# The last product of a fused attention and two-FFN kernel on scaled 16-bit parts, its third batch with seven products for eight

## Chip, cores and metric

The kernel runs on one core of one Trainium2 chip. The metric is the device time of one execution in microseconds; lower is better. Three runs of the kernel before took 1029.26, 1030.34 and 1037.39 us (median 1030.34).

## The reference, cut to what matters

```python
B, H, S, D = 4, 8, 576, 64                 # attention, batch by batch
x = attention_with_memory(q, k, v, M_prev, z_prev, beta)      # (2304, 512)
h = ((x @ w1) * (x @ w2)) @ w3             # 512 -> 1024 -> 1024
x2 = h @ w_out                             # 1024 -> 512
hg = sigmoid(x2 @ w_gate) * (x2 @ w_val)   # 512 -> 1536
out = hg @ w_out2                          # 1536 -> 512, float32
```

The result must hold to float32, so each product is made of parts: an operand is split into a high part and the small rest, and three matmuls are summed (high with high, low weight with high, high weight with low).

## The kernel before, in words

The work goes batch by batch (four of 576 tokens; a row of a result is a tile of 128 features by 576 tokens, in two halves of 288). Weights are converted from 64-bit integers once, in batch 0; w3 and w_out are first multiplied into one matrix. Each batch then has four stages. "ab": eight rows f of `x@w1` and `x@w2`, multiplied into `h`. "xw": four rows of `x2`. "gv", the gate stage: twelve rows of the gate and value products, joined with a sigmoid into `hg`. "ot", the output stage: four rows d, each two halves of 12 feature blocks times 3 matmuls (`prod`, L467), so 4 x 2 x 12 x 3 = 288 matmuls of 288 columns a batch, on 4-byte parts (float32 rounded for TensorE, "fp32r"). The attention of the next batch is woven in between the matmuls of ab, xw and ot by `drive` (L1109), not in gv; batch 3 has none left.

The parts are 4-byte in batch 0. The weights of ab and gv are split again into two 16-bit parts ("late" work, `late_split`, L279): each conversion task loads a raw copy from DRAM into a tile `wraw`, multiplies it by a power of two (`split_scaled`, L174: ACT writes the high part, DVE the rest) and stores it. "P" tasks make plain parts, "S" tasks first form four sums of blocks (`sums`). Batches 2 and 3 use these sums in `two_rows` (L509): seven block products in place of eight (`prod2`, L478), each six matmuls of 288 columns, added up by DVE, ACT and POOL. How often a task's step comes is set by `PACE`, one step in so many calls of `pump`; tasks that a load needs are forced (`late_until`).

Weights reach TensorE through a ring of five tiles `wslot` (`load_step`, L382), loaded by SP's queue in the order of the list `again`; in the third pass the three `wraw` tiles serve as more places. Accumulators: three banks `ps_f`, and four others that the attention uses. PE's order is that of the program (a manual schedule); DVE, ACT, POOL and SP are put in order by a scheduler with its own time model.

The rows of `hg` are split into 4-byte parts by `split_rows` (L569): an ACT cast and a DVE or POOL subtraction. The output row is copied by ACT (L758) and stored by one DMA:

```python
for k in range(F2):
    prod(ps[:, :HS], slot(s + k // 4), k % 4, hs[k], c0, k == 0, k == F2 - 1)
...
nc.scalar.copy(osb[:, c0 : c0 + HS], ps[:, :HS])
```

Of the kernel before, what the change touches and what calls it, by code (L numbers as in the profile page):

```python
# [54 lines left out]
FRAC = 0.96  # L55
FA = (1.0, 0.6)
FR0 = (0.75, 1.0)
PACE = (5, 4, 4, 14, 4)
# [5 lines left out]
def tile_attention_memory_ffn(  # L64
# [35 lines left out]
    mcol = cp.tile([128, NJ + 2 * B], BF16, name="mcol")  # L100
# [20 lines left out]
    def behind(ins):  # L121

        if "pe" in paced:
            tc.add_manual_dep(
                ins.ins,
                paced["pe"].ins.name,
                mybir.DependencyInfo(mybir.DependencyClass.NoSync, mybir.DependencyReason.DATA),
                reason="pace",
            )
# [35 lines left out]
    def total(col, name):  # L165
        n = col.shape[1]
        ps = ps_f.tile([128, 512], F32, tag="f", name=name)
        nc.tensor.matmul(ps[:, :n], ones, col, start=True, stop=True)
        return ps[:, :n]

    def largest(dst, src, axes):
        nc.vector.tensor_reduce(dst, src, axes, ALU.max, apply_absolute_value=True)
# [61 lines left out]
    NTHIRD = len(again)
    again += second
# [12 lines left out]
    done = []  # L248

# [25 lines left out]
    def late_scales():  # L275
        power(wsc[:, :NJ], wsc[:, NJ:], total(mcol[:, :NJ], "wsum"))
        nc.vector.tensor_reduce(wmax, wtop.rearrange("p d f -> p f d"), AX.X, ALU.max)

    def late_split():  # L279
# [5 lines left out]
        m = jobs.index(u)  # L285
        by = wsc[:, m : m + 1]
        raw = raws[n]

        def made(x):
            d = whole16[u][x]  # L290
            nb = d.shape[2]
# [3 lines left out]
            nc.sync.dma_start(out=d, in_=t)  # L295
# [34 lines left out]
    def conv_step():  # L330
# [27 lines left out]
        elif ws["step"] == 1:  # L358
# [3 lines left out]
            nc.vector.scalar_tensor_tensor(z, y, 3, tmp["r"], ALU.logical_shift_left, ALU.bitwise_or)  # L362
            if hf == 1 and u in kept:
                nc.sync.dma_start(out=kept[u], in_=raws[u])
            if hf == 1 and u in whole16:
                n = jobs.index(u)
                largest(mcol[:, n : n + 1], raws[u], AX.XY)
# [14 lines left out]
    def load_step():  # L382
# [3 lines left out]
        src, key, nb = again[m]  # L386
        late = m - NTHIRD
# [3 lines left out]
        while key is not None and key not in done:  # L391
            late_until(ws["task"] + 1)
        n = ws["ring"]
        if key is not None:
            w = fp.tile([128, 2, nb, 128], F16, tag=tag, name=f"wslot{n}", bufs=bufs)
            nc.sync.dma_start(out=w, in_=src[:, :, :nb])
        else:
            w = fp.tile([128, 2, 4, 128], F32R, tag=tag, name=f"wslot{n}", bufs=bufs)
            nc.sync.dma_start(out=w.bitcast(F32), in_=src)
        put(tag, [w])  # L400
# [74 lines left out]
    def prod2(ps, w, blk, x):  # L475
        for k in range(2):
            for part, (wi, xi) in enumerate(((0, 0), (1, 0), (0, 1))):
                paced["pe"] = nc.tensor.matmul(  # L478
                    ps, w[:, wi, blk + k, :], x[:, xi, k, :],
                    start=k == 0 and part == 0, stop=k == 1 and part == 2,  # L480
# [4 lines left out]
    def token_steps(name, x01, x23, ops, scale):  # L485
        both = {}
        b11, b12 = x01[:, :, :HS], x01[:, :, HS:]
        b21, b22 = x23[:, :, :HS], x23[:, :, HS:]
# [759 lines left out]
```

## Time and profile before

| | us |
|---|---|
| median of three runs | 1030.34 |
| the profiled execution | 1028.78 |
| its span, first to last instruction | 1026.8 |
| PE busy in the span | 1000.1 |
| DVE, ACT, POOL busy | 684.5, 571.8, 247.4 |

The trace is that of one execution. PE is TensorE's matmuls, PEld its weight loads, DVE VectorE, ACT ScalarE, POOL GpSimd, SP the engine that issues DMAs. A matmul's own duration contains its way through the array; how fast matmuls follow each other is read from a run of them, its length over its count.

### The profile page before, as it was taken

What the parts mean: (1) busy time and instruction counts of PE and PEld (TensorE: products, weight loads), DVE (VectorE), ACT (ScalarE), POOL (GpSimd) and SP (SyncE); (2) the same over time, 40 slices, a digit from 0 to 9 for tenths busy, and PEclk for the clock granted to TensorE, in tenths of its full rate; (3) what the DMA queues carried; (4) which work ended last, traced back from release to release, by engine and by line L of the source; (5) the groups of instructions that cost most, each with busy time, mean ns of one, the idle gap of its engine ahead of it and who ended that gap; (6) DMA issues with size and microseconds to landing.
All of it is one profiled execution on the core that took longest, in us unless ns stands there. A gap on an engine that the chain in (4) does not pass through costs nothing.

```text
span 1026.8 us, 19856 instructions
## 1 busy us (share of the span) xinstructions
PE 1000.1 (97%) x7382; PEld 834.0 (81%) x7382; DVE 684.5 (67%) x1596; ACT 571.8 (56%) x1179; POOL 247.4 (24%) x246
## 2 busy tenths in 40 slices
PE   7999999999999998999999999899999999999998
PEld 3556787888999898898977788677877888897798
DVE  6865888778776627765566659998877427837730
ACT  7977786567777635654455444455644433235420
POOL 3454021212000201321101012453244302403420
PEclk9989999999999999999999999999999999999999
DMA  8865799857776479863777588655755335545551
GB/s 294 249 214 197 260 345 314 307 193 262 243 248 223 159 252 372 293 201 99 266 245 243 207 282 311 187 182 162 226 179 187 112 112 190 196 150 162 186 193 56
DMA packets 80376, 224.83 MB, mean 219 GB/s; under 512 B 10520, under 2 KB 22936, under 8 KB 80280
## 3 DMA queue, kind: packets, MB, share of 16 engines
q1 hardware_dynamic: 80280, 223.57, 64.2%
q8 instruction: 58, 0.95, 0.4%
q14 instruction: 38, 0.31, 0.1%
HBM read 165.34 MB, written 58.20 MB: 218 GB/s over the span
## 4 chain that ended last, share of the span: by engine, by line
PE 76%; DVE 6%; ACT 2%; issue 1%; DMA 1%; POOL 0%; SPq 0%; DVEq 0%; ACTq 0%; POOLq 0%
PE gv L467 14%; PE ot L467 14%; PE gvp L478 12%; PE ab L467 9%; PE xw L467 9%; PE abp L478 6%; PE s L902 3%; PE t L963 3%; PE o L1031 3%; PE o L1016 1%; PE wps L467 1%; PE o L1024 1%; DMA wraw<-kf 1%; DVE p L907 1%; PE qt L1000 0%
## 5 line engine op out<-in xcount | busy, mean ns | idle before, releaser
L478 PEld LDWEIGHTS <-wslot 128*128 128x128 f16 x1680 | 163.0, 98 | 47.3 <-issue 5.9
L933 POOL TENSOR_SCALAR p<-p,sm,omg 116x116 f32<-116x116 f32 (+4 forms) x100 | 87.3, 877 | 325.4 <-DVE sm L931 187.2
L467 PE MATMUL ot<-hg,wslot 128*128 128x288 f32 x1152 | 165.7, 299 | 0.0
L467 PEld LDWEIGHTS ot<-hg,wslot 128*128 128x128 f32 x1152 | 154.5, 188 | 6.5 <-issue 5.5
L467 PE MATMUL gv<-x,wslot 128*128 128x288 f32 (+1 forms) x1152 | 147.5, 290 | 0.2 <-ACT gsb L134 0.2
L478 PE MATMUL gvp<-x,wslot 128*128 128x288 f16 x1008 | 124.3, 286 | 1.1 <-DVE x L177 1.1
L467 PE MATMUL ab<-x,wslot 128*128 128x288 f32 x768 | 121.0, 308 | 0.2 <-DVE wpart L597 0.2
L134 ACT ACTIVATE p<-p,sm 116x116 f32<-116x116 f32 (+4 forms) x160 | 92.9, 583 | 43.7 <-DVE sm L907 43.5
L467 PE MATMUL xw<-h,wslot 128*128 128x288 f32 x768 | 113.7, 300 | 2.4 <-ACT h L570 1.1
L467 PEld LDWEIGHTS ab<-x,wslot 128*128 128x128 f32 x768 | 107.2, 193 | 7.9 <-issue 5.0
L467 PEld LDWEIGHTS xw<-h,wslot 128*128 128x128 f32 x768 | 103.6, 188 | 7.4 <-issue 3.0
L907 DVE CUSTOM_DVE_ANT_0 p<-s,msk 116x116 f32<-116x116 f32 (+4 forms) x160 | 67.9, 454 | 36.1 <-PE s L902 35.5
L478 PE MATMUL abp<-x,wslot 128*128 128x288 f16 x672 | 87.4, 286 | 1.7 <-DVE c11ab L544 1.2
L572 DVE TENSOR_TENSOR wslot<-wraw,wslot 128x512 fp32r<-128x512 f32 x76 | 56.1, 740 | 40.3 <-ACT wslot L570 40.0
L467 PEld LDWEIGHTS gv<-x,wslot 128*128 128x128 f32 x576 | 76.4, 188 | 0.5 <-ACT gsb L134 0.5
L963 PE MATMUL t<-idf,p 116*116 116x116 f32 x480 | 67.6, 270 | 6.4 <-DVE p L933 3.9
L963 PEld LDWEIGHTS t<-idf,p 116*116 116x116 f32 x480 | 53.6, 137 | 20.7 <-issue 5.2
L467 PEld LDWEIGHTS <-wslot 128*128 128x128 f16 x576 | 56.3, 98 | 14.2
L353 ACT ACTIVATE cy<-r 128x512 f32<-128x512 f32 x76 | 51.3, 675 | 12.0 <-DVE wraw L362 2.4
L570 ACT CAST wslot<-wraw 128x512 fp32r<-128x512 f32 x76 | 47.0, 620 | 17.3 <-PE gv L467 7.4
L362 DVE SCALAR_TENSOR_TENSOR wraw<-cy,cr 128x512 int32<-128x512 int32 x76 | 54.0, 738 | 2.5 <-ACT cr L354 2.3
L981 ACT COPY pt<-t 116x696 f32<-116x696 f32 (+2 forms) x74 | 47.2, 647 | 9.5 <-PE t L963 9.2
(156 smaller groups left out, 1550.5 us busy)
## 6 DMA issues: line engine op xcount, KB each, us to landing
wslot<-k SPq DMA_DIRECT2D x76, 512.0 KB, 4.2
wslot<-ka SPq DMA_DIRECT2D x40, 512.0 KB, 4.0
k<-wslot SPq DMA_DIRECT2D x36, 512.0 KB, 3.7
wraw<-kf SPq DMA_DIRECT2D x32, 512.0 KB, 6.6
wslot<-kb SPq DMA_DIRECT2D x40, 384.0 KB, 3.9
r<-in_gv_dram SPq DMA_DIRECT2D x24, 512.0 KB, 5.2
kf<-wraw SPq DMA_DIRECT2D x20, 512.0 KB, 3.2
ka<-wS SPq DMA_DIRECT2D x20, 512.0 KB, 4.9
```

Source lines behind the costliest of these rows:

```text
L134: ins = nc.scalar.activation(**kw)
L353: nc.scalar.activation(out=y, in_=hi, func=AF.Prelu, scale=2.0**-112, alpha=2.0**32)
L362: nc.vector.scalar_tensor_tensor(z, y, 3, tmp["r"], ALU.logical_shift_left, ALU.bitwise_or)
L467: paced["pe"] = nc.tensor.matmul(ps, w[:, wi, blk, :], x[:, xi, cols : cols + n], start=first and part == 0, stop=last and part == 2,)
L478: paced["pe"] = nc.tensor.matmul(ps, w[:, wi, blk + k, :], x[:, xi, k, :], start=k == 0 and part == 0, stop=k == 1 and part == 2,)
L570: nc.scalar.copy(dst[:, 0], src)
L572: eng.tensor_sub(dst[:, 1], src, dst[:, 0].bitcast(F32))
L902: nc.tensor.matmul(os_[hh], q_[r, 0, i * T : (i + 1) * T], k_[r, 1, c0:c1], start=x == 0, stop=x == len(terms) - 1,)
L907: nc.vector.tensor_tensor_reduce(out=ps_[hh][:, c0:c1], in0=os_[hh], in1=msk[:, SP - w + c0 : SP - w + c1], scale=-0.125, scalar=3.0e38 if ...
L933: lower(SHARE_N).tensor_scalar(ps_[hh][:, :w], ps_[hh][:, :w], sm[:, 6 + hh : 7 + hh], omg[:T, 2 * p + hh : 2 * p + hh + 1], ALU.mult, ALU ...
L963: nc.tensor.transpose(tp[:T, c : c + T], src[hh][:, j * T : (j + 1) * T], idf[:T, :T])
L981: nc.scalar.copy(to, got)
```

## The change

The output stage of batches 1, 2 and 3 uses 16-bit parts scaled by powers of two. `w_out2` gets late tasks of its own: six P and six S (named `("o", dp, g)`), whose raw copies are the 12 `ko` stores that take the place of 12 stores of 4-byte parts. The scale of `hg` comes from a bound (`measure`, `hg_scale`), known after gate row 2: one matmul with a column of ones (`hgsum`) and some DVE instructions on single columns. `hg` is split with `split_scaled`, rows 0 and 1 later through a `queue`. In batches 1 and 2 the loop stays plain, and the copy multiplies by the scale back (`oback`); output goes out by halves. In batch 3 `out_rows` makes two pairs of output rows with seven products of three groups g of four feature blocks: 2 x 7 x 3 x 6 = 252 matmuls. The first pair (dp 0) holds seven banks, so that the seven products of group 0, then of group 1, then of group 2 follow each other; its weights lie ready in three tiles `ow` in the attention's old buffers. A group's operands are 11 `token_steps` on tiles 576 wide: seven splits (p0 to p6) and four subtractions (t1 to t4), queued when the group's four rows are done and let go two in a row. `two_rows` also changes in ab and gv: products 2, 7 and 3 are added into the banks of 1, 6 and 5, so that the sum `c11` on DVE becomes an ACT copy (or goes into the sigmoid), and the sum `u4` on POOL goes. The ring stays at five in the third pass.

```diff
-PACE = (5, 4, 4, 14, 4)
+PACE = (4, 4, 4, 14, 4, 8, 4)
...
+tasks = [(u, "P") for u in jobs[:F2]] + [(("o", *x), "P") for x in pairs_of]
+tasks += [(u, "PS") for u in jobs[F2:]]
+tasks += [(u, "S") for u in jobs[:F2]]
+tasks += [(("o", *x), "S") for x in pairs_of]
...
-        tag, bufs = ("wslot", RING) if late < 0 or late % (RING + 3) < RING else ("wraw", 3)
-        if in_use(tag) >= bufs:
+        if in_use("wslot") >= RING:
             return False
...
-        p2 = product(2, 1, 2, 5)
+        product(2, 1, 2, 5, a)
         c11 = tmp_("asb", "c11")
-        nc.vector.tensor_add(c11, p2, s1)
-        gate(c11)
+        if sigmoid:
+            act_fn(out=c11, in_=a, func=AF.Sigmoid, scale=by)
+        else:
+            nc.scalar.copy(c11, a)
...
+        every = ((0, 0), (1, 1), (2, 2), (3, 5), (4, 3), (5, 4), (6, 6))
+        for g in range(2):
+            for i, xo in every if views else every[:3]:
+                product(i, g, xo)
...
+            for t, d in ((pa, o16[0]["P"][:, 0:3]), (pb, o16[0]["S"][:, 0:3]), (pc, o16[0]["S"][:, 3])):
+                behind(nc.sync.dma_start(out=t, in_=d))
...
+            if f < 2:
+                queue.append(lambda: split_tied(ht[:, 0], ht[:, 1], hraw, hgs[:, 0:1]))
+            else:
+                split_scaled(ht[:, 0], ht[:, 1], hraw, hgs[:, 0:1])
...
+                    first = [steps[x] for x in ("p0", "t1", "p1", "t2", "p2")]
+                    then = [steps[x] for x in ("p5", "t3", "p3", "p4", "t4", "p6")]
+                    queue.extend(first + then)
...
+        flush(len(queue))
+        if b == 3:
+            yield from out_rows(b, 0, hs, oback, views)
+            yield from out_rows(b, 1, hs, oback)
...
+                if b:
+                    nc.scalar.activation(out=osb, in_=ps[:, :HS], func=AF.Copy, scale=oback[:, 0:1])
```

First place, DVE at the end of batch 3. Before, its last six instructions finish gate row 11 (`u3`, `u4` sums, `hgraw` the row):

```order
L544 TENSOR_TENSOR c11gv_11_12507<-gvp_11_2_12500,s1gv_11_12478 128x288
L549 TENSOR_TENSOR u3gv_11_12517<-gvp_11_7_12510,u2gv_11_12487 128x288
L553 TENSOR_TENSOR u4gv_11_12498<-gvp_11_3_12519,u4gv_11_12498 128x288
L559 TENSOR_TENSOR u3gv_11_12517<-u3gv_11_12517,gvp_11_4_12529 128x288
L525 SCALAR_TENSOR_TENSOR hgraw_11_12468<-s5gv_11_12496,x2back_11441,u4gv_11_12498 128x288
L525 SCALAR_TENSOR_TENSOR hgraw_11_12468<-u3gv_11_12517,x2back_11441,c11gv_11_12507 128x288
```

Now the list goes on; `hq_8`, `hq_10` are the four quarters of group 2, `hg_1_m`, `hg_2_m` the 16-bit parts of groups 1 and 2 (a tile holds two operands and bears the even or first one's name, so the two rows that write `hg_2_2` are p3 from `hq_8_1`, then p2 from `hq_8_0`):

```order
L181 SCALAR_TENSOR_TENSOR hg_1_6_12530<-hq_6_0_12094,hgs_11876,hg_1_6_12530 128x576
L564 TENSOR_TENSOR hq_8_0_12237<-hq_8_1_12238,hq_8_0_12237 128x576
L181 SCALAR_TENSOR_TENSOR hg_2_5_12543<-hq_10_0_12380,hgs_11876,hg_2_5_12543 128x576
L181 SCALAR_TENSOR_TENSOR hg_2_5_12543<-hq_10_1_12381,hgs_11876,hg_2_5_12543 128x576
L564 TENSOR_TENSOR hq_8_1_12238<-hq_10_1_12381,hq_8_1_12238 128x576
L181 SCALAR_TENSOR_TENSOR hg_2_0_12533<-hq_8_0_12237,hgs_11876,hg_2_0_12533 128x576
L564 TENSOR_TENSOR hq_8_0_12237<-hq_10_1_12381,hq_8_0_12237 128x576
L181 SCALAR_TENSOR_TENSOR hg_2_2_12540<-hq_8_1_12238,hgs_11876,hg_2_2_12540 128x576
L564 TENSOR_TENSOR hq_10_0_12380<-hq_8_0_12237,hq_10_0_12380 128x576
L181 SCALAR_TENSOR_TENSOR hg_2_2_12540<-hq_8_0_12237,hgs_11876,hg_2_2_12540 128x576
L181 SCALAR_TENSOR_TENSOR hg_2_6_12552<-hq_10_0_12380,hgs_11876,hg_2_6_12552 128x576
L670 SCALAR_TENSOR_TENSOR u2ot_0_12655<-otf_2_12558,hgs_11876,s1ot_0_12654 128x288
```

What moved: of the 11 steps of group 2, p2's low part has become the last but one; the queue had it fifth.

Second place, DVE in row 3 of batch 2's ab stage, with the attention's score rows (ISA, `p`, `sm`) between. Before:

```order
L549 TENSOR_TENSOR u3ab_3_8184<-abp_3_7_8167,u2ab_3_8132 128x288
L907 ISA p_0_4_0_8152,sm_0_4_8154<-s_0_4_1_0_8174,msk,sm_0_4_8154 116x290
L907 ISA sm_0_4_8154 116x1
L907 ISA p_0_4_1_8153,sm_0_4_8154<-s_0_4_1_1_8175,msk,sm_0_4_8154 116x290
L907 ISA sm_0_4_8154 116x1
L820 TENSOR_TENSOR qkl_1_8260<-qk_1_7827,qkh_1_8259 128x580
L553 TENSOR_TENSOR u4ab_3_8143<-abp_3_3_8186,u4ab_3_8143 128x288
L525 SCALAR_TENSOR_TENSOR hraw_3_8101<-s5ab_3_8141,undo_7755,u4ab_3_8143 128x288
L377 TENSOR_TENSOR wraw_27_7690<-wraw_27_7690 128x256
L559 TENSOR_TENSOR u3ab_3_8184<-u3ab_3_8184,abp_3_4_8206 128x288
```

Now:

```order
L620 TENSOR_TENSOR u3ab_3_8260<-abp_3_6_8205,s1ab_3_8203 128x288
L1174 ISA p_0_4_0_8229,sm_0_4_8231<-s_0_4_1_0_8250,msk,sm_0_4_8231 116x290
L1174 ISA sm_0_4_8231 116x1
L1174 ISA p_0_4_1_8230,sm_0_4_8231<-s_0_4_1_1_8251,msk,sm_0_4_8231 116x290
L1174 ISA sm_0_4_8231 116x1
L1087 TENSOR_TENSOR qkl_1_8335<-qk_1_7919,qkh_1_8334 128x580
L624 TENSOR_TENSOR u2ab_3_8212<-abp_3_5_8214,u2ab_3_8212 128x288
L594 SCALAR_TENSOR_TENSOR hraw_3_8181<-s5ab_3_8221,undo_7848,u2ab_3_8212 128x288
L433 TENSOR_TENSOR wrawl_7785<-wrawl_7785 128x256
L631 TENSOR_TENSOR u3ab_3_8260<-u3ab_3_8260,abp_3_4_8281 128x288
```

What moved: the pair `u3`, `u4` has become `u3`, `u2`, which no longer wait for a sum on POOL, and `c11ab`, which stood some rows ahead of these, is gone from DVE.

Third place, SP's queue where batch 3 passes from xw (`k`) to gv (`ka`, `kb`: S and P weights). Before:

```order
L396 DMA wslot_11417<-ka_138 128x2048
L396 DMA wslot_11431<-kb_139 128x2x768
L396 DMA wslot_11482<-ka_141 128x2048
L396 DMA wslot_11496<-kb_142 128x2x768
L396 DMA wslot_11544<-ka_144 128x2048
L396 DMA wslot_11558<-kb_145 128x2x768
```

Now, from the first weight of gv on:

```order
L450 DMA wslot_11529<-ka_141 128x2048
L450 DMA wslot_11577<-kb_142 128x2x768
L450 DMA wslot_11591<-ka_144 128x2048
L867 DMA ow_11666<-op_182 128x4608
L867 DMA ow_11667<-os_183 128x4608
L867 DMA ow_11668<-os_183 128x1536
L450 DMA wslot_11640<-kb_145 128x2x768
L450 DMA wslot_11654<-ka_147 128x2048
```

What moved: the three `ow` loads (128 x 4608, 4608 and 1536 elements of two bytes) stand ahead of the weights of gate row 1.

## Rows read from the trace of the kernel before

**Rows 1.** The page's busy times, whole span: busy us (share) and instructions of each engine.

```profile
PE 1000.1 (97%) x7382; PEld 834.0 (81%) x7382; DVE 684.5 (67%) x1596; ACT 571.8 (56%) x1179; POOL 247.4 (24%) x246
```

**Rows 2.** Windows by stage: start:end, length, then as the second line says.

```profile
core 0: us, PE busy (x) PEld busy (x) DVE busy (x) ACT busy (x) POOL busy (x), PEclk, DMA share, GB/s
...
398.00:471.00 73.00, 73.00 (x555) 63.71 (x554) 51.75 (x127) 41.43 (x89) 20.84 (x17) 0.98 0.70 241
...
503.95:574.60 70.65, 70.65 (x579) 56.50 (x577) 48.15 (x80) 37.85 (x54) 4.20 (x3) 1.00 0.73 245
...
574.60:629.20 54.60, 54.60 (x420) 47.99 (x419) 36.47 (x82) 25.17 (x45) 5.17 (x5) 1.00 0.78 269
...
629.20:697.00 67.80, 64.31 (x515) 47.16 (x513) 63.01 (x167) 33.94 (x81) 33.44 (x33) 1.00 0.64 212
...
796.00:855.00 59.00, 59.00 (x455) 51.19 (x453) 25.38 (x77) 26.43 (x55) 11.47 (x10) 1.00 0.37 119
...
922.70:984.80 62.10, 61.81 (x506) 49.23 (x504) 44.79 (x93) 32.31 (x62) 25.25 (x28) 1.00 0.55 183
...
984.80:1026.80 42.00, 38.44 (x291) 38.21 (x288) 1.45 (x4) 4.41 (x10) 1.67 (x2) 1.00 0.31 104
```

**Rows 3.** Timeline of PE, batch 3: start us, duration us, engine, line, operation, tiles, count.

```profile
903.52 0.18 PE L168 MATMUL x2sum<-mcol,ones 128*128 128x1 bf16 x1
...
927.84 57.24 PE L478 MATMUL gvp<-x,wslot 128*128 128x288 f16 x466 [0.29 <-DVE x L177]
...
984.83 38.42 PE L467 MATMUL ot<-hg,wslot 128*128 128x288 f32 x288
```

**Rows 4.** Waits of PE, whole span: total us, times, longest us.

```profile
PE t L963 <- DVE mn L849: 2.4, 1, 2.4
...
PE abp L478 <- DVE c11ab L544: 1.2, 1, 1.2
```

**Rows 5.** Groups of instructions by form, whole span: busy us, mean ns.

```profile
L467 PEld LDWEIGHTS ot<-hg,wslot 128*128 128x128 f32 x1152 | 154.5, 188 | 6.5 <-issue 5.5
...
L478 PEld LDWEIGHTS <-wslot 128*128 128x128 f16 x1680 | 163.0, 98 | 47.3 <-issue 5.9 <-DMA wslot<-k 0.5
...
L177 DVE SCALAR_TENSOR_TENSOR wS<-wraw,wsc,wS 128x1024 f16<-128x1024 f32 x20 | 26.0, 1300 | 5.9 <-ACT wS L176 5.7
...
L177 DVE SCALAR_TENSOR_TENSOR x<-x2f,x2s,x 128x576 f16<-128x576 f32 x14 | 11.1, 818 | 4.7 <-ACT x L176 4.7
...
L380 DVE TENSOR_TENSOR wraw<-wraw 128x256 f32<-128x256 f32 x20 | 9.7, 484 | 0.3
...
L177 DVE SCALAR_TENSOR_TENSOR wP<-wraw,wsc,wP 128x1024 f16<-128x1024 f32 x12 | 16.7, 1402 | 9.5 <-ACT wP L176 9.4
```

**Rows 6.** The same view, DVE in 629.20 to 697.00 us.

```profile
L544 DVE TENSOR_TENSOR c11ab<-abp,s1ab 128x288 f32<-128x288 f32 x8 | 3.6, 447 | 0.2 <-PE abp L478 0.2
```

**Rows 7.** Timeline of DVE at the end of batch 3's gate stage.

```profile
985.19 0.45 DVE L559 TENSOR_TENSOR u3gv<-u3gv,gvp 128x288 f32<-128x288 f32 x1 [0.28 <-PE gvp L478]
...
985.58 0.52 DVE L525 SCALAR_TENSOR_TENSOR hgraw<-s5gv,x2back,u4gv 128x288 f32<-128x288 f32 x1
...
986.01 0.51 DVE L525 SCALAR_TENSOR_TENSOR hgraw<-u3gv,x2back,c11gv 128x288 f32<-128x288 f32 x1
```

**Rows 8.** Groups of DVE by form, 922.70 to 984.80 us.

```profile
L500 DVE TENSOR_TENSOR x2f<-x2f,x2f 128x576 f32<-128x576 f32 x1 | 0.7, 747 | 0.0
```

**Rows 9.** Timeline of DVE between batches 0 and 1; in brackets the idle time before.

```profile
381.74 1.28 DVE L177 SCALAR_TENSOR_TENSOR wP<-wraw,wsc,wP 128x1024 f16<-128x1024 f32 x1 [4.18 <-ACT wP L176]
...
387.67 1.29 DVE L177 SCALAR_TENSOR_TENSOR wP<-wraw,wsc,wP 128x1024 f16<-128x1024 f32 x1 [4.64 <-ACT wP L176]
```

**Rows 10.** DMA: GB/s in 40 slices of the span; issues, KB each, us to landing.

```profile
GB/s 294 249 214 197 260 345 314 307 193 262 243 248 223 159 252 372 293 201 99 266 245 243 207 282 311 187 182 162 226 179 187 112 112 190 196 150 162 186 193 56
...
wraw<-kf SPq DMA_DIRECT2D x32, 512.0 KB, 6.6
```

**Rows 11.** The output copies (tile osb): ns min/median/max, first and last start us.

```profile
L758 ACT COPY osb<-ot x32: 377/399/402, 344.5 to 1023.3; 128x288 f32<-128x288 f32 x32
```

More of the change, by code (lines that the diff above doesn't have):

```diff
@@ L248, in tile_attention_memory_ffn, with flush @@
     done = []
+    queue = []
+    def flush(n):
+        while queue and n > 0:
+            queue.pop(0)()
+            n -= 1
     def in_use(tag):
@@ L479, in prod2, with split_tied, token_steps @@
                     ps, w[:, wi, blk + k, :], x[:, xi, k, :],
-                    start=k == 0 and part == 0, stop=k == 1 and part == 2,
-                )
-    def token_steps(name, x01, x23, ops, scale):
+                    start=not more and k == 0 and part == 0, stop=k == 1 and part == 2,
+                    skip_group_check=more,
+                )
+    def split_tied(hi, lo, src, by, tied=True):
+        a, d = split_scaled(hi, lo, src, by)
+        if tied:
+            behind(a)
+            behind(d, "dve")
+    def token_steps(name, b11, b12, b21, b22, ops, scale, tags, apart=False, tied=False):
         both = {}
-        b11, b12 = x01[:, :, :HS], x01[:, :, HS:]
-        b21, b22 = x23[:, :, :HS], x23[:, :, HS:]
+        t = {1: b11, 2: b11, 3: b12, 4: b21}
         def parts(m, src):
@@ L509, in two_rows, with sub, step @@
-    def two_rows(s, x, name, ht, hraw, by, sigmoid, cost=0.0):
+                    both[m // 2] = fp.tile([128, 2, 2, 2, HS], F16, tag=tags[m // 2], name=f"{name}_{m}", bufs=1)
+                o = both[m // 2][:, m % 2]
+                split_tied(o[:, 0], o[:, 1], src(), scale(), tied)
+                ops[m] = o
+            return step
+        def sub(n, a, b):
+            def step():
+                if apart and n < 3:
+                    t[n] = fp.tile([128, 2, HS], F32, tag="hraw", name=f"{name}_t{n}")
+                ins = nc.vector.tensor_sub(t[n], a(), b())
+                if tied:
+                    behind(ins, "dve")
+            return step
@@ L658, in ffn @@
             x2 = {}
[L659 removed]
+            x2top = fp.tile([128, 8], F32, tag="x2top", name=f"x2top{b}", bufs=1)
+            steps = token_steps(f"x2_{b}", *quarters(*xf), x2, lambda: x2s[:, 0:1], [f"x{n}" for n in range(4)])
             x2s = bound_x2(b, htop)
@@ new lines, in measure @@
+        def measure(f):
+            if f == 0 and b == 1:
+                for d in range(2):
+                    largest(x2top[:, d : d + 1], x2[d][:, 0], AX.X)
+            elif f == 1 and b == 1:
+                for d in range(2, KC):
+                    largest(x2top[:, d : d + 1], x2[d][:, 0], AX.X)
+            elif f == 0:
+                for n, m in enumerate((0, 1, 5, 4)):
+                    queue.append(
+                        lambda n=n, m=m: behind(largest(x2top[:, 2 * n : 2 * n + 2], x2[m][:, 0], AX.X), "dve")
+                    )
+            elif f == 2:
+                return hg_scale(b, x2top[:, : 4 if b == 1 else 8], x2s)
```

403 lines of the change are left out of this document (297 added, 106 removed).

## The prediction

> **What bounds the kernel now.** I read first how busy each engine is, then where TensorE waits, then single stages. PE is busy 1000.1 of 1026.8 us [rows 1]. The windows by stage say the same closer to the change: in batch 1's gate stage (503.95 to 574.60), batch 1's output stage (574.60 to 629.20) and batch 2's output stage (796 to 855) PE has no idle time at all, DVE is busy for 25.4 to 48.2 us of them, and the granted clock is 1.00, that is 2.4 GHz [rows 2]. So these stages last as long as their matmuls take to follow each other, and the first question is what one matmul costs there, not how busy another engine is. What PE waited for is little: the longest single wait, 2.4 us, is a transpose of the attention that waited for DVE just after batch 0 [rows 4]. One stage stands out: 629.20 to 697.00, batch 2's ab stage, where PE idles 3.5 us (67.80 less 64.31) and DVE is busy 63.0 of 67.8 us [rows 2]. There DVE is the bound beside PE.
>
> **The spacing of matmuls.** The timeline of PE in batch 3 has two long runs with nothing between: 466 gate matmuls on 16-bit parts in 57.24 us, 122.8 ns each, and 288 output matmuls on 4-byte parts in 38.42 us, 133.4 ns each; both have 288 columns [rows 3]. The weight load of the 4-byte form lasts 188 ns, longer than that spacing; that of the 16-bit form lasts 98 ns [rows 5]. The Trainium skill, "TensorE: Matmul & The Clock Gate", section "Back-to-back issue gap", gives a warm spacing of N/2.4 + 2.5 ns with no word of the type, 122.5 ns for 288 columns; by that rule new types alone gain nothing here. The 16-bit run agrees with it (122.8), the 4-byte run doesn't (133.4), and the runs decide the sum below.
>
> **The sum, part by part.**
>
> Batches 1 and 2: 288 matmuls each keep their number and lose 133.4 - 122.8 = 10.6 ns each: 3.05 us a batch, 6.1 us. Attention is woven in there and keeps its own matmuls; PE has no idle time to absorb the gain.
>
> Batch 3: 288 x 133.4 = 38.4 us becomes 252 x 122.8 = 30.9 us: 7.5 us less. Together 13.6 us.
>
> Single-column matmuls: three `hgsum`, `osum` and a second `wsum`. The one like them, `x2sum`, lasts 0.18 us [rows 3]; five cost between 0 (overlapped) and 0.9 us. I take 0.4.
>
> Batch 3, the steps of group 2. While gate rows 4 to 11 run, DVE has per row four sums of 0.45 and two products of 0.52 us [rows 7] and two queued steps, each a split of 0.82 [rows 5] or a subtraction of 0.75 [rows 8]: 2.84 + 1.64 = 4.5 us, against 42 x 0.1228 = 5.16 us of matmuls. It keeps up, but steps of group 1 are left over, and the order now puts p2 of group 2 behind nearly everything. DVE read the last gate product 0.36 us after the first output matmul had started (985.19 against 984.83) [rows 3, 7]; product 7 of the last row comes two products of 0.737 us earlier, so DVE can start `u3` 1.11 us before the output stage. From there to the end of p2 the order has 21 instructions: 11 splits (9.0), 5 subtractions (3.75), three sums and two products (2.4), 15.2 us. Two instructions that follow each other overlap a little: 985.58 to 986.01 is 0.43 for one of 0.52 [rows 7]. With 20 x 0.08 off, p2 is done 12.5 us into the stage, without it 14.1. PE wants that part after 16 products and two matmuls, 98 x 0.1228 = 12.0 us. The wait is 0.4 to 2.0 us; I take 1.0. Nothing in the second product pair hides it, since PE's order is fixed and all its matmuls stand behind.
>
> Batch 3, the `ow` loads. They are 128 x 10752 elements of two bytes, 2.75 MB, 7.4 us at the best rate of any slice, 372 GB/s [rows 10], and row 1's weights stand behind them in SP's queue. The weight ahead of them gets its ring place when the third xw row is done, 48 x 0.1334 = 6.4 us before gv. So they end 1.0 us into gv, and row 1's first weights are wanted at 5.16. If these land as promptly as they can, nothing waits; if they take the 6.6 us of a raw load [rows 10] from there, PE waits 2.4. Bounds 0 and 2.5; I take 0.5. That the ring has five places in the third pass too costs nothing: two places a row of 5.16 us is what the second pass lives on.
>
> The end: the last result was an ACT copy of 0.40 us [rows 11], now a DVE instruction like that at 985.58, 0.52 us [rows 7]: +0.1, then a store as before.
>
> Batch 2's ab stage. Eight `c11ab` sums of 0.447 us [rows 6] leave a DVE that was 93% busy there, and 16 POOL sums go in ab. `c11ab` was also the one named in a 1.2 us wait of PE [rows 4]. The stage can gain between 0 and all 3.5 us of idle time; but the attention's score chain on DVE stays, so I take 1.0.
>
> Other stages. Six P tasks, 1.40 us of DVE each [rows 5], lie in batch 1's ab and xw; there DVE has 73.0 - 51.8 = 21 us free in ab alone [rows 2]. Batch 1's `hg` splits add 12 x 0.06 us and the three rows that POOL did, about 3 us, in a stage with 22 us of DVE free. Six S tasks, at most 4 x 0.48 + 1.30 = 3.2 us each [rows 5], 19 us, lie in batch 2's output stage, with 33.6 us of DVE free. This cover hides their length, not their place: DVE works in order, and a task that waits for its raw load holds what is behind it. Between batches 0 and 1 it stood still so for 4.18 and 4.64 us [rows 9], of which PE felt little. The `pace` and the removal of 12 stores shift these waits: from -2.4 (the longest wait gone [rows 4]) to +4.6 (one such standstill paid in full). I take +0.5.
>
> Sum: -13.6 + 0.4 + 1.0 + 0.5 + 0.1 - 1.0 + 0.5 = -12.1 us, from the profiled execution's 1028.78. That one lies below all three runs shown; two of these lie together, mean 1029.8, 1.0 us above it. I put the sum on that: 1017.7 us.
>
> **Rivals.**
>
> New waits eat half. If the hand-over from ACT to DVE adds 0.6 us to each queued step, a gate row of batch 3 needs 5.7 us of DVE against 5.16, 0.54 us on eight rows, 4.3 us, and p2 comes 1 us later still: 1023. For it: DVE's margin is 0.66 us a row. Against it: ACT has the lighter load in that stage, 32.3 of 62.1 us against DVE's 44.8 [rows 2], so its part should be done first.
>
> More gained than summed. Batch 2's 3.5 us vanish (2.5 more than taken) and the 2.4 us wait goes (2.9 more than taken): 1012.3. For it: POOL's and DVE's relief falls just there. Against it: the score chain is untouched.
>
> The change does not do what it says for the types: 16-bit products keep the 133.4 ns of the output stage, so only 36 matmuls go, 4.8 us, and with the same additions 1.5: -3.3, 1026.5. Against it: the 16-bit gate run of 466 shows 122.8 with the same columns and banks [rows 3]. The skill's rule named above would end near this too, since it leaves only the 36 matmuls.
>
> Slower. The 12 new tasks stand in DVE's order between pieces of attention, each behind a raw load. If each costs PE 2.4 us, as the worst wait did [rows 4], that is 28.8 us: 1046. It turns the sign when six of the twelve do so. Against it: before, 20 such tasks cost PE one such wait.
>
> **How the numbers follow.** Forecast 0.55, its own range 1014.5 to 1021; half eaten 0.22; more gained 0.13; types without effect 0.05; slower 0.05. All the upper ends of the terms together give -3.5 us, 1026.3; all the lower ends -19.0, 1010.8. So the range is 1011 to 1026, which leaves out the slower case and the edges. One per cent, about what a measurement of this kernel can tell, is 1020.0 us. Faster by more: 0.49 of the forecast and the 0.13, 0.62. Within 1%: 0.06 of the forecast, 0.22 and 0.05, 0.33. Slower by more: 0.05.
>
> **What would show it.** In the profile after: batch 1's and 2's output matmuls as 16-bit forms, long runs at 122.8 ns; 252 output matmuls in batch 3 in 31 to 33 us; one PE wait of 0.4 to 2 us on a DVE split of `hg` some 12 us into that stage; no wait on a DMA in batch 3's first gate rows; less PE idle time in batch 2's ab stage. Wrong would be: a spacing of 133 ns on 16-bit parts; PE idle between gate rows 4 and 11 of batch 3; several waits of PE for attention rows in batch 1.

## The result and the profile after

The changed kernel takes 1018.81 us (median of four runs, 1017.02 to 1020.62) against 1030.32 beside it: a ratio of 0.9874, 95% interval 0.9824 to 0.9924, so about 11.5 us or 1.1% faster. The forecast was 1017.7. The profiled execution is one of the two longer ones, 1020.42 us with a span of 1018.6; the changed kernel was therefore profiled a second time on another chip (1017.8 us, span 1016.0), and stages are read from both.

The page's busy times after, beside [rows 1]:

```profile
PE 990.1 (97%) x7351; PEld 800.3 (79%) x7351; DVE 731.5 (72%) x1702; ACT 596.7 (59%) x1213; POOL 194.5 (19%) x196
```

PE is busy for 10.0 us less; DVE works 47 us more, POOL 53 less. PE is still the bound. The windows of the stages that the prediction spoke of, columns as in [rows 2]: batch 1's gate and output, batch 2's ab and output, batch 3's gate, and the end.

```profile
504.79:575.38 70.59, 70.59 (x580) 56.39 (x578) 51.98 (x90) 39.17 (x55) 0.00 (x0) 1.00 0.78 267
575.38:627.89 52.51, 51.19 (x420) 37.27 (x418) 35.86 (x79) 26.85 (x46) 5.00 (x5) 1.00 0.66 216
627.89:687.59 59.70, 58.45 (x482) 43.11 (x479) 53.92 (x147) 34.22 (x85) 24.64 (x23) 1.00 0.68 224
792.42:851.48 59.06, 57.00 (x465) 40.66 (x462) 43.14 (x108) 32.27 (x61) 10.07 (x10) 1.00 0.52 162
919.35:983.62 64.27, 62.30 (x507) 49.24 (x506) 48.97 (x103) 31.46 (x63) 9.39 (x12) 1.00 0.56 193
983.62:1018.60 34.98, 31.33 (x254) 24.55 (x251) 17.80 (x29) 9.91 (x16) 2.95 (x4) 0.99 0.24 80
```

The difference of a row's length and its PE busy time is what PE waited for. Before, the two output stages had none; now they have 1.32 and 2.06 us, so PE's work there shrank by more than the lengths say. To compare stages, each is measured on PE's timeline from its first matmul to the first of the next (us; the last two columns are the second profile of the changed kernel and the second one of the version with three edits, below):

| stage | before | after | after, again | three edits |
|---|---|---|---|---|
| batch 1 ab | 85.14 | 81.08 | 81.36 | 80.81 |
| batch 1 output | 54.76 | 52.51 | 52.52 | 51.04 |
| batch 2 ab | 62.35 | 59.70 | 59.58 | 59.84 |
| batch 2 gate | 62.74 | 64.70 | 64.72 | 64.93 |
| batch 2 output | 60.20 | 59.06 | 59.07 | 58.27 |
| batch 3 gate | 62.11 | 64.27 | 63.44 | 63.39 |
| batch 3 output, to the end | 41.96 | 34.94 | 34.94 | 34.94 |
| all the rest | 597.5 | 602.3 | 600.4 | 600.5 |

Of these seven stages all but batch 3's gate repeat within 0.3 us. The rest does not: it holds batch 0, where stretches of lower granted clock come and go from one execution to the next (220 to 240 us: 0.81 and 0.85 in the first profile after, 0.93 and 0.89 in the second, 1.00 before). It is also longer than before in both: batch 1's first matmul starts 385.9 us into the one profile of the kernel before, and 387.9 to 392.1 us into all twelve profiles of the changed kernel and its variants. Single stages therefore tell more here than the total.

The waits of PE after (total us, times, longest), beside [rows 4]:

```profile
PE xsum L172 <- DVE bcol L1056: 1.9, 2, 1.3
PE gvp L532 <- ACT x L180: 1.6, 2, 0.8
PE gvp L532 <- DVE x L181: 1.4, 3, 0.5
PE abp L532 <- DVE u2ab L603: 1.1, 2, 0.7
...
PE gvp L532 <- DMA wslot<-kb: 0.7, 1, 0.7
```

The 2.4 us wait for `mn` is gone, and so is the one for `c11ab`. In their place stand a wait of the single-column matmul `xsum` for its DVE operand in each of the two output stages, and waits for the split `x` in the gate stages of batches 2 and 3. Before, `x` cost 0.44, 0.32 and 0.29 us there; now 1.6 + 1.4.

`xsum` is not new. The kernel before has it in the same two stages, without a wait (first fence). What is new is what stands on DVE ahead of its operand `bcol`: two subtractions of the attention's tail, `x_t` and `xp`, which the change moved there (second fence, batch 1's output stage after).

```profile
613.78 0.18 PE L168 MATMUL xsum<-mcol,ones 128*128 128x1 bf16 x1
```

```profile
611.30 0.75 DVE L564 TENSOR_TENSOR x_t<-xp,x_t 128x576 f32<-128x576 f32 x1
611.96 0.75 DVE L564 TENSOR_TENSOR xp<-xp,xp 128x576 f32<-128x576 f32 x1
...
612.97 0.15 DVE L1056 TENSOR_REDUCE bcol<-xmax 128x1 bf16<-128x4 f32 x1
```

Batch 3's output stage on PE's timeline, and the DVE split that it waited for, beside [rows 3] and [rows 7]:

```profile
983.62 2.50 PE L654 MATMUL otf<-hg,ow 128*128 128x288 f16 x18
...
996.12 0.65 PE L654 MATMUL otf<-hg,ow 128*128 128x288 f16 x4 [0.20 <-DVE hg L181]
...
999.54 15.60 PE L654 MATMUL otp<-hg,wslot 128*128 128x288 f16 x126
```

```profile
995.25 0.81 DVE L181 SCALAR_TENSOR_TENSOR hg<-hq,hgs,hg 128x576 f16<-128x576 f32 x1
```

126 matmuls of the second pair take 15.60 us, 123.8 ns each with the last one's end in it. The single wait comes 12.5 us into the stage, on group 2's p2, and lasts 0.20 us.

### The profile page after: what moved, and what is told of

Same layout as the page of the kernel before. It is cut to its first block, busy times and chain, and to the rows that moved or that the text cites. A ratio compares the mean times of both kernels' runs of the same rounds, so it can differ in the third digit from the quotient of the medians.

```text
span 1018.6 us, 19895 instructions
## 1 busy us (share of the span) xinstructions
PE 990.1 (97%) x7351; PEld 800.3 (79%) x7351; DVE 731.5 (72%) x1702; ACT 596.7 (59%) x1213; POOL 194.5 (19%) x196
## 5 line engine op out<-in xcount | busy, mean ns | idle before, releaser
L532 PEld LDWEIGHTS <-wslot 128*128 128x128 f16 x1680 | 162.8, 98 | 51.0 <-issue 8.7
L521 PEld LDWEIGHTS <-wslot 128*128 128x128 f16 x1152 | 110.8, 98 | 34.0 <-issue 6.6
L521 PE MATMUL ot<-hg,wslot 128*128 128x288 f16 (+1 forms) x864 | 119.3, 291 | 0.0
L521 PE MATMUL ab<-x,wslot 128*128 128x288 f32 x768 | 118.3, 302 | 0.5 <-ACT asb L800 0.4
L521 PEld LDWEIGHTS ab<-x,wslot 128*128 128x128 f32 x768 | 104.2, 188 | 8.4 <-issue 4.9
L1230 PE MATMUL t<-idf,p 116*116 116x116 f32 x480 | 69.7, 274 | 2.8 <-DVE p L1200 2.2
L402 ACT ACTIVATE cy<-r 128x512 f32<-128x512 f32 x76 | 51.4, 676 | 10.8 <-issue 2.2
L1298 PE MATMUL o<-pt,vs 116*64 116x344 f32 (+2 forms) x320 | 51.7, 417 | 0.5 <-ACT pt L1248 0.5
L521 PE MATMUL wps<-wo,wslot 128*128 128x512 f32 x192 | 52.2, 407 | 0.0
```

The source lines that it names most:

```text
L402: nc.scalar.activation(out=y, in_=hi, func=AF.Prelu, scale=2.0**-112, alpha=2.0**32)
L521: paced["pe"] = nc.tensor.matmul(ps, w[:, wi, blk, :], x[:, xi, cols : cols + n], start=first and part == 0, stop=last and part == 2,)
L532: paced["pe"] = nc.tensor.matmul(ps, w[:, wi, blk + k, :], x[:, xi, k, :], start=not more and k == 0 and part == 0, stop=k == 1 and part == 2,
L1230: nc.tensor.transpose(tp[:T, c : c + T], src[hh][:, j * T : (j + 1) * T], idf[:T, :T])
L1298: nc.tensor.matmul(ot[r, XO + q0 : XO + S], v_[:, j, hh], pt[:, hh, j].rearrange("p a c -> p (a c)")[:, q0 - X : S - X] if j < 4 else pt[: ...
```

## The experiments

All of them compute the whole result; each changes only what its diff shows. Times are medians; the ratio is to the kernel before on the same chip.

**Eight products on 16-bit parts in batch 3.**

```diff
-        if b == 3:      # output by seven products
+        if b == 9:
...
-        for d in range(KC if b < 3 else 0):
+        for d in range(KC):
```

> Batch 3's output stage back to eight products, but on 16-bit parts: 288 matmuls instead of 252, no loads of the seven products' weights, no steps group by group. If the two halves of batch 3's gain add as forecast (10.6 ns of spacing on each matmul, and 36 matmuls of 122.8 ns fewer), the stage from its first output matmul to the end of the span is longer than the changed kernel's 34.98 us by 36 x 0.1228 = 4.4 us, less the 0.2 us wait on the second part of group 2: about 39.2 us; the whole kernel 3 to 4.5 us longer than the changed one. Rival: the gain comes from the order of the steps, not from the number of products; then the stage stays within 1 us of 34.98. Second rival, types without effect: the eight products follow each other at 133 ns, and the stage is back at 41.97 us.

1023.92 us, ratio 0.9896 (0.9859 to 0.9933). PE's timeline of the stage:

```profile
983.81 35.44 PE L521 MATMUL ot<-hg,wslot 128*128 128x288 f16 x288
```

From there to the end of the span it is 39.13 us: 4.2 more than the changed kernel, as expected, and 2.8 less than before (3.05 by the spacing). 35.44/288 is 123.1 ns. So both halves of batch 3's gain are shown, and both rivals fall.

**Batches 1 and 2 back on 4-byte parts.**

```diff
-            s = take(2 if b else 3)
+            s = take(3)
...
-            ht = fp.tile([128, 2, S], F16 if b else F32R, ...)
+            ht = fp.tile([128, 2, S], F32R, ...)
```

> Batches 1's and 2's output stages back on 4-byte parts, 12 slots each, with the gate's rows split as before; batch 3 stays as changed. Theory, spacing by type: 133.4 ns instead of 122.8 on 288 matmuls, so each of the two stages is 3.05 us longer (net of waits: batch 1's from 51.2 to 54.2, batch 2's from 57.05 to 60.1), the kernel 5 to 6 us longer, minus at most 1.9 if the waits for a reduced row sum there go too. Rival: these stages got shorter because splits left them or because the clock stood better; then both stages stay within 1 us.

1027.2 us, ratio 0.9934 (0.9912 to 0.9957). The two output stages, columns as in [rows 2]:

```profile
577.24:633.19 55.95, 54.85 (x421) 48.21 (x419) 36.98 (x81) 26.34 (x46) 5.06 (x5) 1.00 0.73 245
797.76:859.15 61.39, 60.46 (x465) 52.08 (x463) 42.51 (x108) 31.70 (x61) 11.64 (x11) 1.00 0.62 201
```

PE is busy for 54.85 and 60.46 us where it was 51.19 and 57.00 with 16-bit parts: 3.66 and 3.46 more, where 3.05 was expected. The longest uninterrupted stretch in this run confirms the spacing itself:

```profile
617.19 16.16 PE L521 MATMUL ot<-hg,wslot 128*128 128x288 f32 x120
633.19 0.91 PE L532 MATMUL abp<-x,wslot 128*128 128x288 f16 x6
```

From start to start that is 16.00/120 = 133.3 ns. The 0.4 to 0.6 us beyond 288 x 10.6 ns may lie where output matmuls alternate with the attention's; no run isolates it.

**Batch 3's first pair without the group order.**

```diff
-            for i, xo in every if views else every[:3]:
+            for i, xo in every[:3]:
...
-            for g in range(2 if views else 0, 3):
+            for g in range(0, 3):
```

> Batch 3's first row pair product by product, with three products on group 0 and 1 ahead, instead of group by group over all seven; the sums are the same. Theory, the order over seven banks is what gives DVE time for the parts of group 2: all of group 2's parts are wanted after 7 to 9 products of three matmuls less than 42 x 2 in front, so TensorE waits in the first 12 us of the stage for 2 to 6 us, and the end is later by as much. Rival, DVE would have been in time anyway: no wait over 0.5 us there, and the time within 1 us of the changed kernel's 1018.8.

1026.91 us, ratio 0.9943 (0.9918 to 0.9968). The stage is 43.6 us long against 34.9. PE's timeline, then windows of it:

```profile
982.80 5.54 PE L654 MATMUL otf<-hg,ow 128*128 128x288 f16 x42
990.33 0.59 PE L654 MATMUL otf<-hg,ow 128*128 128x288 f16 x2 [1.99 <-ACT hg L180]
992.37 1.12 PE L654 MATMUL otf<-hg,ow 128*128 128x288 f16 x4 [1.45 <-DVE hg L181]
994.75 0.64 PE L654 MATMUL otf<-hg,ow 128*128 128x288 f16 x2 [1.25 <-ACT hg L180]
995.60 1.12 PE L654 MATMUL otf<-hg,ow 128*128 128x288 f16 x4 [0.22 <-DVE hg L181]
996.51 6.61 PE L654 MATMUL ots<-hg,ow 128*128 128x288 f16 x36
```

```profile
988.00:990.33 2.33, 0.34 (x4) 0.13 (x3) 2.33 (x5) 1.94 (x3) 0.00 (x0) 1.00 0.00 0
990.33:992.37 2.04, 0.59 (x2) 0.25 (x2) 2.01 (x4) 0.74 (x1) 0.00 (x0) 0.52 0.00 0
...
996.51:999.70 3.19, 3.19 (x15) 1.98 (x14) 0.52 (x1) 0.00 (x0) 0.79 (x1) 0.50 0.00 0
999.70:1002.95 3.25, 3.25 (x24) 2.41 (x23) 0.52 (x1) 0.00 (x0) 0.00 (x0) 0.85 0.13 45
1002.95:1005.16 2.21, 2.21 (x21) 1.76 (x18) 0.52 (x1) 0.00 (x0) 0.80 (x1) 1.00 0.04 7
```

The theory holds: DVE isn't in time for a product-by-product order, and the waits sum to 4.91 us. The loss is 8.6, though. The windows show the remainder: from the end of the first of these waits on the granted clock is 0.52 to 0.50, the lower of the two levels, and it is back at 1.00 only about 1 us into the window from 999.70 on, by that window's mean of 0.85. The 36 matmuls on `ots`, 4.4 us at 122.8 ns, take 6.61.

**Batch 2's ab sums as before.**

```diff
-            nc.scalar.copy(c11, a)            # products 1 and 2 in one bank
+            nc.vector.tensor_add(c11, p2, s1)
...
-        nc.vector.tensor_add(u2, c, u2)
+            nc.gpsimd.tensor_add(u4, u2, s5)  # and p3 added on DVE
```

> Only the row pair's sums of the ab stages are put back: c11's sum as an instruction of DVE, u4 on POOL. Theory, DVE's relief is what took 2.65 us off batch 2's ab stage: it returns from 59.7 to 61 to 62.4 us with 2 to 3 us of idle TensorE time, and the wait on c11's sum (1.2 us before) is back; the kernel 1 to 3 us longer. Rival, the stage got shorter by a better place of the attention's tasks: it stays within 0.7 us of 59.7 and the idle time near 1.1.

1025.63 us, ratio 0.9926 (0.9898 to 0.9954). The stage's window, and PE's waits in it:

```profile
625.54:690.58 65.04, 58.91 (x481) 43.09 (x479) 57.52 (x155) 31.64 (x77) 30.12 (x31) 1.00 0.62 207
```

```profile
PE abp L532 <- DVE c11ab L614: 3.0, 2, 1.9
PE t L1266 <- DVE p L1236: 3.0, 2, 1.7
```

The stage is 5.3 us longer than after, twice the upper end of what was expected, and 2.7 longer than before the change; batch 3's ab stage adds 0.9. So the new sums of the ab stages are worth 6 us, and the rest of the change takes 2.7 us back in batch 2's ab stage. Which part of the rest does that was not isolated. Nor is it shown that DVE's load alone is what the new sums relieve: with the old ones DVE is busy for 57.52 us and not 53.92, but POOL also for 30.12 and not 24.64, and each of the seven products has an accumulator bank of its own again. Of the waits on `c11ab`, the one of 1.2 us falls on a row's seventh product, which with three banks takes the one that the sum `c11` reads.

**x_6's split ahead of the table load.** Two columns of Sigmoid are computed in the last xw row of batches 2 and 3, and the first sigmoid of the gate is ordered behind ACT's split of x_6.

```diff
+            if b > 1 and d == KC - 1:
+                pre = fp.tile([128, 2], F32, tag="pre", ...)
+                act_fn(out=pre, in_=x2s, func=AF.Sigmoid)
```

> One edit in the third pass's gate stages: the split of x_6 on ACT is tied ahead of the first sigmoid, and the sigmoid's table is loaded by a two-column activation in the last xw row, so that the table load no longer stands ahead of that split. Theory: the 2 us by which batch 2's and batch 3's gate stages grew (64.70 and 64.27 against 62.74 and 62.11) come from that load of 1.28 us and the c11 sigmoid ahead of the split: in both stages the waits on ACT's and DVE's x go from 2.0 and 1.3 us to under 0.5, and each stage is 0.8 to 1.5 us shorter. Rival, the new sums of hg in these gate rows or SP's queue hold the rows up: the stages stay within 0.4 us. The kernel by the theory 1.5 to 3 us below the changed one.

1018.59 us, ratio 0.9880 (0.9864 to 0.9897). The reason for the edit is ACT's order in batch 3's first gate row, before (first fence) and after (second):

```profile
926.04 0.78 ACT L176 ACTIVATE x<-x2f,x2s 128x576 f16<-128x576 f32 x1 [0.45 <-DVE x2f L500]
926.83 1.28 ACT L134 ACT_TABLE_LOAD   x1
```

```profile
922.24 1.28 ACT L137 ACT_TABLE_LOAD   x1
923.54 0.50 ACT L137 ACTIVATE c11gv<-gvp,x2back 128x288 f32<-128x288 f32 x1
923.94 0.76 ACT L180 ACTIVATE x<-x2f,x2s 128x576 f16<-128x576 f32 x1
```

Now that c11's sigmoid needs no DVE sum, it is ready first and takes the load of its table with it, and the split of x_6 starts 4.59 us into the stage in place of 3.32, 1.3 us later. With the edit PE's timeline has in batch 3 (first two rows), and in batch 2:

```profile
923.03 0.65 PE L533 MATMUL gvp<-x,wslot 128*128 128x288 f16 x4 [0.30 <-DVE x L181]
924.75 2.50 PE L533 MATMUL gvp<-x,wslot 128*128 128x288 f16 x19 [1.06 <-DMA wslot<-kb]
...
733.15 4.09 PE L533 MATMUL gvp<-x,wslot 128*128 128x288 f16 x30 [1.17 <-DVE x L181]
```

In batch 3 the theory holds for the waits: 0.81 and 0.45 become one of 0.30, what it was before the change (0.29). But the stage is 63.50 us long, no shorter than in the changed kernel's second profile (63.44): PE now waits 1.06 us for row 1's weights instead (taken up below). In batch 2 the theory falls: 0.76 + 0.50 turn into 1.17, and the stage stays at 64.93. What is late there is DVE: three sums of a weight block (0.41, 0.43, 0.41) and a sum of the products (0.45) stand ahead of the split, and the split itself takes 1.34 us in place of 0.82 (the last section). The kernel as a whole is not the expected 1.5 to 3 us shorter.

**Two empty steps in the tails.**

```diff
-            first, run("t1", "t2", "t3"), lambda: finish_x(b, mx),
+            first, run("t1", "t2", "t3"), lambda: None, lambda: None, lambda: finish_x(b, mx),
```

> One edit in the tails of the softmax: two empty steps stand between the reduction of the row maxima and the step that uses them. Theory: the changed order left that step too close behind, so TensorE waited 1.32 us in batch 1's and 0.61 us in batch 2's output stage for DVE; these two waits go, about 1.9 us in all, and nothing else moves. Rival, DVE is late as a whole there: the waits stay at 1 us and more in sum, or reappear one step later under another name.

1015.67 us, ratio 0.9854 (0.9836 to 0.9873). The output stages are 51.04 and 58.28 us, 1.48 and 0.78 shorter, and the waits for `bcol` are gone. The first one's window:

```profile
575.82:626.86 51.04, 51.04 (x420) 37.27 (x418) 35.20 (x79) 26.63 (x46) 4.99 (x5) 1.00 0.66 217
```

PE busy equals the length again; the theory holds, and the 2.26 us are a little more than the 1.93 expected. One more stage moved than expected: batch 3's ab stage is 41.35 us long in place of 41.93.

**The output weights' loads later.**

```diff
-            for t, d in (...three loads...): behind(nc.sync.dma_start(out=t, in_=d))
+                if 2 <= f < 5:   # one of them in each of gate rows 2, 3, 4
```

> One edit: the three loads of the seven products' output weights are issued one each in gate rows 2, 3 and 4 of batch 3 instead of ahead of that stage. Theory: row 1's weights no longer stand behind 2.75 MB, so the 0.70 us wait of TensorE on that load goes, and the output stage still finds its weights there; the kernel 0.3 to 0.8 us shorter, which only the list of waits can show. Rival: the wait moves to a later row's weights with the same 0.7 us or more.

1020.96 us, ratio 0.9903 (0.9880 to 0.9926). No wait of 0.2 us or more on a DMA is left in batch 3's gate stage, but its length is 63.39 us, that of the changed kernel's second profile (63.44), and the total shows no gain. The profiles of the ab and the tails edit, which leave these loads where they were, have no load wait either, and the one with x_6's split has 1.06 us. What orders these cases is when row 1's weights land. In the two fences, the changed kernel and this run, the last number is the time from issue to landing:

```profile
wslot<-kb SPq DMA_DIRECT2D x1, 384.0 KB, 8.9
```

```profile
wslot<-kb SPq DMA_DIRECT2D x1, 384.0 KB, 3.4
```

Issued 1.4 us ahead of the gate stage, they land 6.5 to 7.6 us into it in all seven profiles with the `ow` loads ahead of them, and 2.0 to 2.2 us into it in the five without. PE wants them at 6.7 where it has waited for x_6 before, and at 5.6 where it has not. So the load wait belongs to the change. The waits for x_6 hide it, all but what comes later than 6.7 (7.56 in the first profile after, 6.72 in the second), and taking these waits away lays it open (6.79, with a wait of 1.06).

**The three edits together, the changed kernel again, and one edit more.**

> The three edits together: x_6's split ahead of the table load, the later tails, the output weights loaded in gate rows 2 to 4. If each theory holds and they add: 1.6 to 3 us in the two gate stages, 1.9 in the two output stages, 0.7 on the load, 4 to 5 us below the changed kernel, 1014 to 1015 us. Rival, the waits are shifted and not removed: within 1.5 us of 1018.8.

1014.16 us, ratio 0.9845 (0.9830 to 0.9860), the expected 1014 to 1015. Its parts are not the expected ones: batch 2's gate stage is 64.93 us, 0.2 longer, batch 3's 62.27, 2.0 and 1.2 shorter than in the two profiles of the changed kernel. In batch 3 two edits that gave nothing alone (63.50 and 63.39) give 1.1 together here, since each took away one of two waits that hid each other. Since its ratio was taken on another chip than the changed kernel's, both ran again side by side.

> The changed kernel itself, on the chip of the two others, so that they can be compared with it there. Two things are open about its first profile: a wait of 0.70 us on row 1's weights in batch 3's gate stage, and 10-us windows at a granted clock under 1.00 in batch 0's xw and output stages. Theory, both differ from one execution to the next: here the load wait is another one or none, and those two stages are back near 38.6 and 50.4 us, while the waits for x_6 (0.81 and 0.45 in batch 3, 0.76 and 0.50 in batch 2) and for the row sum (1.32 and 0.61) stand at the same places with the same lengths. Rival, the load wait belongs to the change: 0.5 to 1 us at the same row again.

> The version with three edits once more, on the same chip as the changed kernel, since the two were on different chips: by the waits removed (0.81 + 0.45 - 0.29 in batch 3's gate stage, 1.32 + 0.61 in the output stages) 2.9 us below the changed kernel; a load wait that comes in some executions adds up to 1. Rival, chip to chip differences made it look faster: within 1 us.

The changed kernel: 1017.58, ratio 0.9864 (0.9830 to 0.9897). Three edits: 1015.02, ratio 0.9837 (0.9801 to 0.9872), 2.6 us below it against 2.9 expected. The intervals overlap; what carries the difference is the two output stages in the table, 51.04 for 52.52 and 58.27 for 59.07, the empty steps' part. Of the gain in batch 3's gate stage this second profile shows none (63.39 for 63.44). The second profile of the changed kernel has batch 3's waits for x_6 at the same place with the same lengths, and no load wait. Of batch 0's two stages the output stage is back at 50.36 us, but xw took 40.07 and not 38.6.

```profile
923.04 0.41 PE L532 MATMUL gvp<-x,wslot 128*128 128x288 f16 x2 [0.82 <-ACT x L180]
923.89 4.36 PE L532 MATMUL gvp<-x,wslot 128*128 128x288 f16 x34 [0.45 <-DVE x L181]
```

The second profile of the three edits has a load wait of 0.94 us three rows later, in row 4, whose weights now stand behind the second of the `ow` loads: that lands 21.13 us into the stage and they at 22.15, and PE wants them at 21.1. In the first profile the two landed at 19.72 and 20.89, and there was no wait. The rival of the run with the later loads is borne out so far: the wait can move to a later row. What the later loads give lies between nothing and 1.1 us, from one execution to the next.

The last edit ties DVE's sums of the weight block behind x_6's split in batch 2:

```diff
+        if "guard" in split:          # set when x_6's split is issued
+            tc.add_manual_dep(i.ins, split.pop("guard").ins.name, ...)
```

> The three edits of the run before together, and one more in batch 2's first gate row: DVE's four sums of a weight block are tied behind the split of x_6. Theory, what is left of batch 2's growth there is these sums: in the run with the split first three of them and a sum of 0.45 stood between x_6's halves' sum and its split, and TensorE waited 1.17 us. It falls to 0.3 to 0.8 us, the gate stage from 64.93 to 64.1 to 64.6, and batch 3's stays at 62.27. Rival, the split waits for ACT and not for DVE's order: 1.0 us and more stays. The kernel 0.3 to 0.9 us below the run before, which only the stage can show.

1016.48 us, ratio 0.9828 (0.9787 to 0.9869). The wait falls from 1.17 to 0.32 as the theory had it:

```profile
733.17 3.67 PE L543 MATMUL gvp<-x,wslot 128*128 128x288 f16 x28 [0.32 <-DVE x L181]
737.06 1.14 PE L543 MATMUL gvp<-x,wslot 128*128 128x288 f16 x8 [0.23 <-DVE u2gv L615]
```

But the stage is 64.66, only 0.27 shorter and just outside the expected 64.1 to 64.6: part of it comes back at once as a new wait of 0.23 for the next row's `u2`, which the moved sums now stand ahead of on DVE. Batch 3's stage is 62.70, with a load wait of 0.26 in row 4. In the total it can't be told. Of all these edits only the two empty steps are shown to be worth having by themselves.

## Why the prediction was right, and where its steps were not

**Spacing by type: right.** As matmul time the terms -3.05 and -3.05 measured -3.57 and -3.15 (lengths 54.76 and 60.20 less 51.19 and 57.05, the lengths after without their waits), and putting the type back cost 3.66 and 3.46. In batch 3, -7.5 measured 38.42 to 31.3 us of matmuls, -7.1. The rival in which types don't matter is refuted by two runs. What failed is the sentence that PE has no idle time to absorb the gain: it had none before, but the two stages themselves became only 2.25 and 1.14 us shorter, since waits came in, `xsum` in both and in batch 2 also the attention's for DVE and ACT (0.72, 0.26 and 0.42 us). With 4-byte parts put back, batch 2's waits are 0.54 and 0.33.

**Batch 3's p2: right in mechanism and place, small in size.** Forecast 0.4 to 2.0 us, taken 1.0; it was 0.20, under the lower end. DVE's last part ended 995.25 + 0.81 - 983.62 = 12.4 us into the stage, the early end of the forecast's 12.5 to 14.1, and PE came there at 12.3 and not 12.0. No wait of 0.2 us or more lies between gate rows 4 and 11: DVE kept up, so the rival with half the gain eaten falls. The run without the group order shows what the order buys: 8.6 us.

**Batch 2's ab stage: mis-sized.** Taken -1.0 within 0 to -3.5; it measured -2.65 and -2.77. That was a sum of two larger numbers: -5.3 for the new sums, +2.7 from the rest. The 3.5 us of idle time were read from a window, 629.20 to 697.00, that runs 5.6 us into the xw stage, whose first matmul is at 691.38; in the 62.35 us of the ab stage PE idled 3.1. The bound by the stage's idle time was no bound for the edit, since the rest of the change would have added idle time.

**Single-column matmuls: right; the wait of `xsum` was in no term.** The five that the prediction counted last 0.17 to 0.18 us each (`x2sum` 0.18 [rows 3]), and PE waits before none of them, so they cost at most the 0.9 us of its upper bound. `xsum` is a sixth that was there before, and the prediction left it out of its sums: the changed order of the tails put two subtractions ahead of its operand, which cost 1.32 + 0.61 us. The run with two empty steps gives them back.

**Other stages: +0.5 was a balance of things not foreseen.** Batch 1's ab stage lost 3.8 to 4.1 us: 2.4 of it is the `mn` wait, which the prediction had as the best end of this term and in the rival with more gained; and before, the clock stood at 0.93 and 0.90 in 390 to 410 us, right around that wait, which is 0.7 + 1.0 us of full clock, and at 1.00 after. There is one profile of the kernel before, and no run puts this wait back. The gate stages of batches 2 and 3 grew by 2.0 and 1.3 to 2.2 us, which no term had: the prediction looked at DVE's load there and not at what a c11 without its DVE sum does to the order of ACT. Nor had any term batch 0, which the change touches by its new stores; the rest of the table grew by 4.8 and 2.9 us, most of it there, and how much of that is the change and how much the clock stays open. The twelve new tasks, the rival on the slower side, cost no visible wait of the size it needed.

**The loads of `ow`: mis-sized, and hidden.** Taken 0.5 within 0 to 2.5. The prediction had the loads end 1.0 us into the gate stage, at the best rate of any slice; they ended 5.4 to 6.5 us into it, and row 1's weights behind them landed at 6.5 to 7.6, against 5.16 when they were to be wanted. PE waited only 0.70 us in one profile and not at all in the other, because x_6 held it until 6.7; where x_6 did not, it waited 1.06.

So the median came out within 1.1 us of the forecast, but only the spacing and the count of the matmuls were foreseen; that the remainder cancelled is luck. By the stages of the two profiles after, the two output stages with attention gave 3.4 us of the 6.1 taken, batch 3's end 7.0, and the ab stages of batches 1 and 2 6.7 and 6.6, of which the sum had 1.0; the gate stages of batches 2 and 3 took 4.1 and 3.3 back and the rest 4.8 and 2.9. That is -8.2 and -10.8 us from the profile before, which itself lies 1.5 us under its kernel's median; the sum said -12.1, and the medians differ by 11.5.

## What to carry to other kernels

Where PE never waits, price a change by the start-to-start spacing in the longest uninterrupted run of each form, not by engine load; then ask what PE will meet when it comes there sooner (batch 2's output stage kept 1.14 of 3.05 us). Where an edit removes an instruction from a chain, look at every engine on which the chain's next instruction is now ready earlier: it may pass something that was more urgent (here a table load passed a split). A reduction that another engine waits for needs distance to its reader, and what is put between eats it (here two subtractions of 0.75 us). Two waits close behind each other hide one another: taking away either gave nothing here, taking away both up to 1.2 us, so look at when the second operand arrives, and not only at the list of waits.

## What was not expected of the hardware

**A wait costs more than its length.** In the run without the group order 4.91 us of waits cost 8.6 us, because the clock fell to its lower level at the end of the first of them, 1.99 us long, and stayed there for about 10 us, as its windows show. The single wait of 1.32 us in batch 1's output stage left the clock at 1.00; no run tells what makes the difference.

**DVE and POOL hold each other up.** In the first run with three edits a split on DVE took 1.34 us beside a POOL sum, and 0.82 elsewhere (first fence). With one edit more the split came first, and the POOL sum (0.83 us in the first fence) and a DVE sum behind it, 0.41 us elsewhere, were stretched (second).

```profile
730.71 0.83 POOL L627 TENSOR_TENSOR s5gv<-u3gv,s5gv 128x288 f32<-128x288 f32 x1 [11.82 <-ACT c11gv L137]
730.80 1.34 DVE L181 SCALAR_TENSOR_TENSOR x<-x2f,x2s,x 128x576 f16<-128x576 f32 x1
```

```profile
732.30 0.82 DVE L181 SCALAR_TENSOR_TENSOR x<-x2f,x2s,x 128x576 f16<-128x576 f32 x1
733.03 1.02 DVE L434 TENSOR_TENSOR wrawl<-wrawl 128x256 f32<-128x256 f32 x1
...
732.51 1.25 POOL L637 TENSOR_TENSOR s5gv<-u3gv,s5gv 128x288 f32<-128x288 f32 x1 [11.57 <-DVE u3gv L632]
```

POOL's sum ends 0.64 us after the split does (733.76 against 733.12), and DVE's next one 0.29 after POOL's (734.05): each seems to do most of its work only once the other is through, though a part must lie ahead of that, since 0.64 and 0.29 are less than the 0.83 and 0.41 that they take alone. The Trainium skill, "SBUF — State Buffer", section "SBUF: two separate sides", has a rule of this kind: a DVE instruction with two inputs in SBUF and a GpSimd instruction that reads SBUF exclude each other at a shared port pair; whichever starts first holds it for its whole length, and the other one waits. These rows agree with it in who waits (the later one) and roughly in how long.
